# Two attentions on one core: the order table of the units is arranged anew

## The chip, the cores and the metric

The kernel runs on one core of a Trainium2 chip. The metric is device time in microseconds (us) from launch to end; less is better. Three runs of the kernel before gave 173.02, 172.65 and 172.67 us, a median of 172.67.

## The reference

Two attentions stand one behind the other. The first takes q, k, v of shape (8 batches, 8 heads, 576 rows, 64), pools k and v eightfold to 72 rows, and attends. Its output, seen as x of shape (8, 576, 512), goes into a mixture of four causal attention experts, of which each row takes the two with the largest gate logits.

```python
k_p = k.reshape(B, H, Sp, 8, D).mean(axis=3)
v_p = v.reshape(B, H, Sp, 8, D).mean(axis=3)
attn = softmax(q @ k_p.T / sqrt(D))
x = heads_side_by_side(attn @ v_p)
logits = x @ w_gate
w = softmax over the two largest logits
for e in range(4):
    a = causal_softmax((x @ wq[e]) @ (x @ wk[e]).T / sqrt(64))
    out += w[e] * (a @ (x @ wv[e]) @ wo[e])
```

## The kernel before

The 576 rows of a batch are worked as 512 main rows and 64 tail rows; the tails of two batches (b-1, b with b odd) are joined to one block of 128 rows. Matmuls are in bf16 with sums in fp32.

The work of each batch is cut into **units**, and a unit's name is `batch:unit`. The main ones:

- loads (`lk`, `lq`, `lv`, with a head group's number in batches 0 and 1; tails `lkt`, `lqt`, `lvt`; weights `W:lq`, `W:lk`, `W:lv`, `W:lo`), all issued on SyncE's queue (SP)
- `ks`, `vs`: first sums of the pooling, on GpSimd (POOL) from batch 2 on, on VectorE (DVE) and POOL before; `kt`, `vt`, `qt`, `qc`: casts to bf16 on POOL (`qc` in batches 0 and 1 on DVE and ScalarE, ACT); `W:c0` to `W:c3`, `W:cv`, `W:co`: casts of the weights on ACT
- `kp`, `vp` (line 362, 378): the pooling ends as matmuls, copied out by DVE
- `q0` to `q3` (396): four transposes, copied out by DVE; `s0` to `s3` (419): scores of the first attention, two 512-wide matmuls with 64 rows of contraction each, then one exponential on ACT (`etA`); `a0` to `a3` (432): eight matmuls, then DVE divides by the sums (`rzA`, `x_tm`)
- `x0` to `x3` (464): transposes of x, copied by DVE; in batches 6 and 7 the DMA does it (`xd`)
- `p0` to `p3` (512): projections to query and key, four 512-wide matmuls with `wqk`, copied out by ACT (`qk`); `v0`, `v2` (527): values and gate logits, eight 260-wide matmuls, copied out by DVE
- `g1` to `g6`: the gates
- `c00`, `c01`, `c10`, `c11`, `c2` (645, 656): scores of the experts, matmuls with 64 rows of contraction, an exponential on ACT and the causal mask on POOL (`etB`, `etC`); `o0`, `o1` (665): twenty matmuls, scaled by DVE; `t0`, `t1` (699, or by DMA in batches 4 to 6): transposes; `w`, `y`, `z` (719, 728): the output projection, copied out by ACT or DVE, and stored
- `qx`, `sx`, `ax`, `xx`, `pt`, `vx`, `h0`, `h1`, `hd`, `ox`, `tx`, `w4` (756 to 960): the same for the joined tails
- `W:h0` to `W:h31` (287): **empty units**, two 512-wide matmuls on a tile of zeros each, whose result is not used.

The units `s`, `c`, `sx`, `h0`, `h1`, `hd` contract over 64 rows, in pairs: one matmul in rows 0 to 63 of the array, one in rows 64 to 127. The profile shows them as `64*128` and this document calls them **row-tiled**; all other matmuls are **full**.

A unit is a Python generator with up to three stages: its matmuls, the reading of their result by ACT or DVE, and what follows (a mask, a store). The string `ORDER` (line 21) names a unit once for each stage. The last lines of the kernel (986 to 991) walk through it:

```python
parts = {}
for name in ORDER.split():
    if name not in parts:
        parts[name] = units[name]() or iter(())
    next(parts[name], None)
```

So the first mention of a unit issues its matmuls, the second the copy or the exponential, the third the mask or the store. Every instruction goes through a wrapper that keeps the program's order (126 to 141; for that reason nearly all lines of the profile are L134), and each engine works off its own in that order. `ORDER` is thus the queue of every engine at once, SP's too. Waits follow from data and from buffers: results of matmuls lie in two rings of PSUM, `ps1` with 2 buffers (`kp`, `vp`, `q`, `x`, `p`, `t`, `w`, `y`, `qx`, `xx`, `pt`, `vx`, `ox`, `tx`, the empty units) and `ps2` with 3 (`s`, `a`, `v`, `c`, `o`, `z`, `sx`, `ax`, `h0`, `h1`, `hd`), lines 145 and 146. A unit that takes a buffer waits until the unit that had it before has been read. The raw inputs have two buffers of each kind (148).

Of the kernel before, what the change touches and what calls it, by code (L numbers as in the profile page):

```python
# [43 lines left out]
3:x1 1:ox 3:x3 3:x1 4:s1 3:x3 W:lo 4:s3 4:s0 4:s3 3:x0 4:vp 3:x0 5:ks 3:pt 3:pt 4:s2 4:vp 5:kt 2:c11
4:s2 3:x2 2:c00 5:q2 2:g3 1:o0 3:x2 2:c11 1:o1 3:p3 4:a3 5:q2 5:q3 3:p3 3:hd 5:lv 5:lvt 1:o1 2:c2
5:q1 5:q3 2:g4 3:p2 4:a3 2:c2 3:hd 4:a0 5:q1 4:a0 5:qt 2:c11 3:p1 2:c2 4:a1 2:c01 3:p2 5:vs 6:lq
4:a1 3:c10 2:c10 3:p1 1:t1 3:vx W:co 3:vx 1:t1 6:lk 3:v0 3:c10 5:q0 3:p0 5:q0 0:w0 4:a2 3:hd 2:c10
3:v0 2:g5 2:c10 3:c11 0:w0 3:h0 5:kp 3:p0 4:a2 5:qx 3:c11 3:v2 5:kp 5:qx 0:w3 3:h0 2:g6 3:v2 0:w3
5:vt 6:lvt 5:s3 5:s1 4:x0 5:s3 1:t0 6:qc 7:lvt 2:o0 4:x0 4:x2 1:t0 5:s1 0:w2 4:x2 2:o0 5:sx 3:g1
0:w2 5:vp 5:vp 3:g2 4:x1 7:kt 5:s0 6:lv 0:w3 5:sx 7:vt 3:c2 2:o1 4:x1 6:q3 6:q3 4:x3 5:s0 4:x3 3:g3  # L50
2:o1 3:c2 5:ax 0:w1 4:p1 5:ax 0:w1 4:p1 2:t0 3:h1 2:t0 6:lkt 7:lk 3:c10 5:s2 6:q1 5:s2 6:q1 5:a0
6:vt 4:p0 6:q0 6:q0 6:ks 4:v2 6:vs 5:a0 3:h1 2:t1 4:p0 2:t1 4:p3 6:kt 1:w3 4:p3 5:a2 5:a1 3:g4 4:p2
7:lq 4:v2 1:w3 5:xx 5:a2 5:a1 4:p2 3:c01 5:xx 3:c00 6:kp 3:c01 3:c00 5:a3 6:kp 5:pt 0:w1 7:ks 6:q2
4:c01 5:a3 6:s3 3:c2 4:c00 6:q2 5:pt 1:tx 0:w2 1:tx 6:vp 5:x0 3:g5 4:c01 4:v0 1:w3 4:c00 5:x0 6:s3
2:w1 6:vp 6:lqt 2:w1 0:w0 5:x1 3:c11 4:v0 6:s1 6:s0 3:g6 5:x1 5:x3 4:g1 7:qc 3:c00 5:x2 5:x3 3:o1
7:lqt 6:s1 4:g2 1:w4 6:a3 6:s0 5:x2 2:w0 3:c01 7:lv 1:w4 2:w0 6:a0 3:o1 6:a3 5:p3 7:q2 4:c2 5:p3
6:a0 4:c00 7:qt 1:w4 7:q2 4:c11 6:s2 7:kp 2:w0 4:c2 6:s2 4:c01 3:ox 7:kp 7:q3 5:v0 7:q3 6:a2 3:ox
2:w2 5:p2 5:v0 4:c11 2:w2 5:vx 4:c10 6:a2 7:vs 7:s3 5:vx 4:c2 6:a1 5:p2 4:c10 1:w2 2:w3 4:g3 5:v2
1:w2 6:a1 5:v2 2:w3 1:w0 3:t1 5:h1 2:w2 7:s3 3:t1 7:s2 5:hd 6:xd0 7:q1 4:c10 7:q1 1:w0 5:h1 5:hd
6:xd3 5:p1 3:o0 1:w0 5:g1 7:vp 3:o0 7:s2 5:c10 4:g4 6:xd1 7:vp 4:g5 5:g2 5:p1 5:c10 4:g6 7:s1 7:s1  # L60
5:g3 7:q0 4:o0 6:xd2 5:p0 7:q0 7:a3 5:g4 5:hd 4:o0 1:w1 7:a1 5:p0 1:w1 7:qx 7:a3 2:w1 7:qx 5:c2 7:a1
7:s0 3:tx 7:s0 6:p3 3:tx 7:a2 2:w3 1:w2 5:c2 6:p1 7:a0 7:a2 7:a0 5:g5 4:c11 1:w1 7:sx 6:p3 5:h0 6:p0
6:v2 6:p1 3:w4 4:t0 5:h0 7:sx 3:w4 6:v2 7:ax 7:xd2 4:o1 6:p2 6:p0 7:ax 3:t0 5:c11 4:o1 6:p2 3:t0
5:c11 7:xd3 5:g6 5:c01 5:c00 7:xd0 3:w3 5:c10 3:y1 3:w3 7:xd1 5:c11 6:v0 3:y1 3:w0 5:c2 6:v0 5:c00
3:w0 5:ox 6:c00 4:t1 5:ox 6:c2 7:xx 5:c01 7:v0 6:g1 6:c2 6:g2 4:w2 3:y1 6:c00 5:o1 7:xx 3:w2 7:v2
# [956 lines left out]
```

## Time and profile before

| | |
|---|---|
| median of three runs | 172.67 us (172.65 to 173.02) |
| span of the profiled execution | 171.8 us |
| time of the runs beside that span | 0.9 us more |
| TensorE matmul (PE) busy | 160.6 us, 94% |
| ACT busy | 125.1 us, 73% |
| DVE busy | 124.3 us, 72% |
| POOL busy | 100.8 us, 59% |
| empty matmuls | 61 records, 18.2 us busy |
| DMA | 42.03 MB, mean 245 GB/s |
| granted TensorE clock | 1.00 |

The profile comes from one execution; its times count from the first instruction, and its span leaves out what lies around the program's instructions, so the runs are a little longer. PE is TensorE's matmuls, PEld its weight loads, which overlap. A row of the timeline gives the start, the length, the engine, line, operation, what is written and read by the program's names, the shape and the number of merged instructions; in brackets stands idle time ahead of it and what ended that. The chain of waits goes back from the last instruction to what released it each time. A matmul's record is longer than the distance to the next matmul's start, since they are pipelined (26 of the 2,090 matmuls have no record).

### The profile page before, as it was taken

To read this page: it belongs to the slowest core of one execution; us is meant where nothing else is said; L and a number is where in the kernel's file an instruction comes from. 1 tells how busy PE (TensorE), PEld (TensorE's weight loads), DVE (VectorE), ACT (ScalarE), POOL (GpSimd) and SP (SyncE) were. 2 spreads that over 40 slices of the span, in tenths; PEclk is the share of its full clock that TensorE was granted. 3 is DMA by queue.
4 is the path that set the end of the run, shared out by engine and by line. 5 is a ranking of instruction groups with operands and counts; after the bars stand their busy time and mean duration, and the time that the engine had idled before them with its cause. 6 is when DMAs were issued, how large, how long until landed. Compare 5 with 4: busy or idle time off the path is not lost.

```text
span 171.8 us, 5246 instructions
## 1 busy us (share of the span) xinstructions
PE 160.6 (94%) x2064; PEld 101.7 (59%) x2090; DVE 124.3 (72%) x358; ACT 125.1 (73%) x176; POOL 100.8 (59%) x222
## 2 busy tenths in 40 slices
...
GB/s 140 262 342 335 306 301 257 332 335 329 216 321 347 332 332 301 295 287 334 302 82 341 360 216 201 230 126 61 67 122 275 65 125 156 210 216 132 333 253 208
DMA packets 52712, 42.03 MB, mean 245 GB/s; under 512 B 21712, under 2 KB 47824, under 8 KB 52688
## 3 DMA queue, kind: packets, MB, share of 16 engines
...
HBM read 30.42 MB, written 9.44 MB: 232 GB/s over the span
## 4 chain that ended last, share of the span: by engine, by line
PE 75%; DVE 7%; ACT 6%; DMA 4%; SPq 3%; issue 2%; DVEq 0%; ACTq 0%
PE p_ps L134 14%; PE v_ps L134 8%; PE y_ps L134 7%; PE sB_ps L134 5%; PE oB_ps L134 5%; PE sA_ps L134 4%; PE qT_ps L134 4%; DMA qraw<-in_q_dram 4%; PE idle_ps L134 4%; PE oA_ps L134 4%; PE xT_ps L134 3%; SPq L134 3%; PE oBt_ps L134 3%; PE vp_ps L134 2%; PE pt_ps L134 2%
## 5 line engine op out<-in xcount | busy, mean ns | idle before, releaser
L134 ACT ACTIVATE etA<-sA_ps 72x1024 bf16<-72x1024 f32 x32 | 31.3, 1018 | 10.7 <-PE sA_ps L134 10.5
L134 PE MATMUL p_ps<-xT,wqk 128*128 128x512 bf16 x114 | 31.5, 379 | 1.5 <-ACT qk L134 0.6
L134 ACT ACTIVATE etB<-sB_ps 128x1024 bf16<-128x1024 f32 x32 | 32.2, 1025 | 0.2 <-PE sB_ps L134 0.2
L134 POOL TENSOR_SCALAR_AFFINE_SELECT etB<-etB 128x256 bf16<-128x256 bf16 x48 | 18.8, 410 | 12.2 <-ACT etB L134 11.8
L134 POOL TENSOR_TENSOR vsum<-vraw 128x512 bf16<-128x512 f32 (+2 forms) x18 | 18.3, 1041 | 9.9 <-DMA vraw<-in_v_dram 9.8
L134 ACT CAST qk<-p_ps 128x512 bf16<-128x512 f32 x32 | 18.5, 586 | 7.6 <-PE p_ps L134 6.8
L134 DVE TENSOR_TENSOR x_tm<-oA_ps,rzA 128x512 bf16<-128x512 f32 x32 | 22.1, 692 | 1.1
L134 PE MATMUL idle_ps<-idle 128*128 128x512 bf16 x61 | 18.2, 414 | 3.1 <-DVE kp L134 1.3
L134 PEld LDWEIGHTS <-wqk 128*128 128x128 bf16 x192 | 14.7, 98 | 10.4 <-issue 1.1
L134 DVE COPY qT<-qT_ps 128x512 bf16<-128x512 bf16 x32 | 15.4, 487 | 6.2 <-PE qT_ps L134 5.9
L134 POOL TENSOR_TENSOR ksum<-kraw 128x512 bf16<-128x512 f32 (+1 forms) x16 | 18.0, 1146 | 2.3 <-DMA kraw<-in_k_dram 2.3
L134 PE MATMUL y_ps<-wo_t,oT 128*128 128x512 bf16 x57 | 16.7, 379 | 0.2
L134 PE MATMUL v_ps<-wvg,xT 128*128 128x260 bf16 x128 | 16.8, 274 | 0.0
L134 ACT COPY ofin<-y_ps 128x512 f32<-128x512 f32 x20 | 11.6, 587 | 6.4 <-PE y_ps L134 1.7
L134 POOL CAST qbf<-qraw 128x2048 bf16<-128x2048 f32 x6 | 11.4, 1897 | 5.6 <-ACT etT L134 5.5
L134 PEld LDWEIGHTS <-xT 128*128 128x128 bf16 x128 | 11.9, 97 | 3.1 <-issue 0.4
L134 PEld LDWEIGHTS <-etA 72*128 72x128 bf16 x256 | 11.0, 97 | 4.3 <-DVE x_tm L134 0.4
L134 PE MATMUL sB_ps<-qk 64*128 64x512 bf16 (+3 forms) x128 | 13.2, 299 | 0.0
L134 PEld LDWEIGHTS <-etB 128*128 128x128 bf16 x256 | 11.3, 97 | 2.5 <-POOL etB L134 0.6
L134 DVE COPY xT<-xT_ps 128x512 bf16<-128x512 bf16 x24 | 9.7, 420 | 4.1 <-PE xT_ps L134 3.8
L134 PE MATMUL oB_ps<-vaug,etB 128*128 128x65 bf16 x256 | 12.4, 193 | 0.1
L134 PE MATMUL qT_ps<-ident,qbf 128*128 128x128 bf16 x128 | 12.2, 219 | 0.3
...
## 6 DMA issues: line engine op xcount, KB each, us to landing
...
```

Source lines behind the costliest of these rows:

```text
L134: return tc.keep_in_program_order(fn(*args, **kwargs))
```

## The change

Only the string `ORDER` changes: the same units, with the same stages, in another order. Nothing is added and nothing taken away; shapes, buffers, engines and the code of the units stay. The new order comes from a search on a model with durations taken from a trace, which charges for each change between full and row-tiled matmuls. Since the table is the order of all queues, the order of the loads changes too, and the places of the empty units. The first 20 lines and the last 6 of the old table, then the first 21 and the last 6 of the new:

```diff
@@ -19,58 +19,58 @@
 ORDER = """
-W:h21 W:h22 W:h7 0:lk3 W:h3 0:lq3 0:lkt 0:ks3 0:kt 0:qc3d 0:lk2 W:h18 0:lk0 W:h14 W:h16 0:lv1 W:h27
-0:lvt 0:qc3a W:h28 0:lq0 W:h13 0:kp3 0:lq2 0:lk1 W:h30 0:q3 0:vs1 1:lq1 0:lq1 0:kp3 0:qc0a 1:lkt
-0:ks2 W:h12 W:h25 0:vt 1:qc1a 0:qc0d 0:lv2 0:q3 0:s3 0:qc2a W:h4 0:s3 0:qc1a 0:vs2 0:ks0 0:kp2 W:h9
-W:h1 0:kp2 0:ks1 1:qc1d 0:qc2d 0:kp0 0:lv3 W:h26 0:kp1 0:kp0 W:h19 0:lv0 W:h15 0:kp1 0:q0 0:vs0 W:h5
-0:qc1d 0:q2 0:q0 1:lq0 W:h8 0:q2 1:kt 0:vs3 0:q1 1:q2 0:q1 0:s0 0:s1 0:s0 0:s2 1:lk1 0:vp 1:q2 0:s2
-1:lk0 1:lvt 0:vp 1:ks1 0:lqt W:h23 1:lv1 1:q3 0:a0 1:lv0 0:a2 1:q3 W:lk 1:qc0d 1:ks0 1:lqt W:h6 0:s1
-0:a1 1:vt W:lq 0:a2 0:a0 1:qc0a 0:a1 W:h29 1:q1 W:h11 W:h17 W:h2 1:q1 1:kp1 1:kp0 1:kp1 1:vs0 1:kp0
-0:a3 1:q0 0:a3 1:s2 1:qt 1:s1 1:q0 W:lv 0:x0 1:s0 1:s2 0:x2 2:lq 1:s1 1:s3 2:qc 1:s0 0:x0 W:c1 0:x2
-0:x1 W:h10 W:h0 1:vs1 W:h20 W:h24 1:s3 0:x3 0:x1 1:vp 0:x3 W:c3 0:p1 2:lkt 1:vp W:c2 0:p1 1:qx 1:qx
-1:a1 1:a3 1:a0 W:c0 0:p3 1:a1 1:sx 1:a3 0:p3 W:cv 2:kt 0:p0 1:a0 2:lk 1:a2 0:p2 0:v2 1:a2 1:sx 0:v0
-0:p0 1:x3 0:p2 0:c2 1:x1 0:v2 0:c2 0:c11 0:v0 1:x3 1:x2 0:c11 0:c2 0:c10 1:x1 2:lv 2:lvt 1:x2 0:g1
-0:c00 0:g2 0:c11 2:q0 2:q0 1:x0 1:x0 1:ax 2:q1 2:q1 1:ax 1:p1 1:p2 0:c00 0:c01 2:ks 3:lk 0:g3 0:g4
-1:v2 3:lkt 1:p1 2:q3 1:v2 2:vs 2:q3 1:p2 2:lqt 2:kp 0:c01 1:v0 3:lqt 1:xx 2:kp 0:g5 3:lq 2:vt 3:lvt
-2:s1 0:c10 0:c10 1:xx 2:s1 1:v0 2:s0 2:q2 1:vx 2:q2 2:s0 2:s3 2:s3 0:g6 2:s2 2:s2 3:lv 2:vp 4:lq
-0:c00 1:vx 1:g1 0:o1 1:g2 2:vp 1:p3 2:a1 1:g3 2:a2 0:o1 3:ks 3:qt 0:c01 2:a1 1:p3 1:pt 2:a2 4:lkt
-2:a0 1:p0 3:kt 1:pt 2:a3 2:a0 2:a3 4:lk 4:lvt 3:qx 1:g4 1:hd 1:h0 3:qx 3:qc 1:p0 1:hd 3:kp 1:h0
-1:c11 3:kp 1:c2 2:x2 2:x1 3:vs 2:x2 3:vt 4:lv 1:c11 2:x1 0:o0 1:c2 2:x0 0:o0 2:x3 1:c00 2:x0 3:sx
-2:x3 1:c00 1:c10 3:q2 3:q3 3:sx 2:v2 4:qc 3:q2 3:q3 0:t1 5:lq 1:c10 1:g5 3:q1 0:t1 4:kt 3:q1 3:s3
-2:v2 2:v0 0:t0 2:v0 3:s3 3:s1 3:s2 0:t0 3:q0 3:s1 1:h1 3:vp 3:q0 2:p1 3:s2 1:hd 4:lqt 3:vp 3:s0
-7:lkt 1:c01 4:q2 2:g1 1:h1 2:g2 1:c00 2:p1 4:q2 3:s0 3:a1 5:lkt 2:p0 4:q1 1:c2 3:a1 4:ks 4:q1 3:a3
...
-7:p0 3:w3 4:y0 5:t1 6:c11 6:g6 7:c11 7:c10 5:t0 6:c00 6:o1 4:y0 5:tx 7:p0 7:c10 7:c11 6:c01 7:p1
-6:o1 4:y1 5:tx 6:o0 5:w4 7:p1 5:y1 7:c11 7:c2 7:g4 4:y0 5:w4 6:t1 7:c00 6:o0 7:c01 5:y1 6:t0 7:c2
-5:y2 7:c10 5:y2 7:pt 5:y1 5:y2 7:c2 7:c01 7:pt 5:y0 7:o1 7:g5 5:w4 7:c01 5:y0 7:g6 7:h1 5:w3 7:o1
-7:c00 6:y1 5:w3 6:y1 7:c00 7:o0 6:w0 7:h1 7:t1 7:h0 5:y0 7:o0 5:w3 7:t1 7:hd 6:w0 7:t0 6:y1 7:hd
-6:w0 6:y3 7:h0 7:hd 7:t0 6:y3 7:z2 6:y3 7:z2 7:ox 7:ox 6:w2 6:w2 7:z0 7:tx 6:w2 7:tx W:h31 7:w4 7:z0
-7:w4 7:w4
+W:h16 W:h27 0:lk3 W:h29 W:h21 W:h24 W:h5 W:h20 W:h22 0:lkt W:h23 0:lk0 W:h18 W:h15 W:h11 0:lq3 0:lq1
+0:ks0 0:lq2 W:h0 W:h6 0:lq0 0:ks3 0:qc3a W:h9 W:h10 0:lk2 0:kt 0:qc3d 0:lv0 W:h3 W:h12 W:h19 0:vs0
+0:q3 0:lv3 0:q3 W:h2 0:lk1 0:kp0 0:ks2 1:lq1 W:h26 0:kp0 0:kp3 W:h4 0:qc0a 0:qc2a 0:qc0d 0:kp3
+0:qc2d 0:lv1 0:lvt 0:qc1a 0:q0 1:qc1a 1:lkt W:h13 0:q0 W:h7 0:vt 0:lv2 0:kp2 1:lk1 1:lk0 0:kp2 1:lv0
+0:qc1d W:h25 W:h1 1:lq0 0:ks1 0:lqt 0:q1 0:q2 0:s3 0:s0 0:q1 1:lv1 0:s3 0:q2 1:qc1d W:h8 0:s2 0:kp1
+0:s2 1:kt 0:kp1 0:vs1 W:h14 0:s0 1:lvt W:h30 0:vs3 0:vs2 1:q3 0:s1 1:q3 0:vp W:h28 0:s1 0:vp 1:q2
+1:ks1 0:a2 0:a0 1:kp1 1:lqt W:lq 0:a2 0:a3 0:a0 1:ks0 0:a1 1:q2 W:lk 1:kp1 W:lv 1:s2 0:a1 1:vs0
+1:kp0 0:a3 1:qc0a 1:kp0 1:s3 1:qc0d 0:x2 1:q1 1:s2 0:x2 1:q0 1:q1 1:s3 1:vt 1:s1 1:q0 0:x1 2:lq 1:s0
+1:qt 1:vs1 2:lk 1:s1 0:x1 2:qc 1:s0 1:vp 0:x0 W:c0 W:c2 1:vp 1:a1 0:x0 1:qx 1:a1 1:a0 2:lkt 1:qx
+1:a3 0:x3 W:c1 0:x3 1:a2 2:lv 1:a3 W:c3 0:p2 2:lvt 4:lvt 1:a0 1:a2 0:p2 1:sx W:cv 0:p0 2:ks 0:p1
+0:v0 2:kt 3:lqt 3:lkt 0:p0 1:x0 0:p1 1:x0 2:lqt 0:v0 0:p3 0:c00 1:sx 0:p3 1:x1 0:c01 0:c11 1:x3
+0:c00 1:x1 1:x2 0:c01 3:lk 0:v2 3:lq 1:x3 2:q1 1:x2 2:q1 2:q0 0:c11 1:v0 2:q0 2:q3 1:p1 1:p1 2:q3
+0:v2 1:ax 0:g1 0:c11 1:v0 1:p2 2:kp 0:g2 0:c2 1:p2 2:vs 1:v2 0:g3 1:ax 2:kp 0:c2 2:s1 1:xx 2:q2 2:vt
+1:v2 0:g4 3:lv 0:c00 1:xx 2:s0 0:c10 3:lvt 2:s1 2:s0 2:q2 1:vx 1:vx 0:c10 4:lq 0:c2 2:vp 0:c10 3:qt
+2:s2 0:g5 2:s2 2:s3 2:vp 1:p3 1:p3 5:lqt 0:g6 2:a1 2:a2 3:kt 1:g1 2:a1 1:pt 2:a2 2:s3 1:c11 2:a0
+1:c11 1:p0 3:ks 2:a0 2:a3 2:a3 4:lkt 0:c01 0:o1 1:pt 3:qx 1:g2 4:lk 0:o1 3:qc 1:p0 1:h0 3:vs 3:kp
+5:lq 3:qx 0:o0 1:h0 1:c10 1:c00 3:kp 1:c10 W:h17 2:x0 1:c00 2:x3 1:hd 0:o0 1:h1 7:lqt 2:x0 5:lkt
+3:q1 4:lv 2:x3 3:vt 1:hd 2:x1 1:h1 1:c2 3:q1 2:x1 1:g3 1:g4 2:x2 3:s1 1:c11 0:t0 2:x2 3:q3 2:v2 4:qc
+0:t0 4:lqt W:lo 3:q0 3:s1 3:q3 4:vt 2:v2 3:q2 3:q2 2:v0 3:s3 2:v0 3:vp 1:c00 7:lvt 1:c2 3:sx 3:q0
+3:s3 1:c01 3:s0 0:t1 3:vp 2:p0 3:sx 3:s0 1:hd 0:t1 5:lvt 3:a1 2:g1 2:p1 2:p0 3:a1 1:g5 4:q2 5:lk
+3:s2 3:ax 4:q2 5:lv 4:q0 4:q0 2:p1 1:c01 4:ks 2:p3 4:q3 3:s2 1:c01 4:kt 3:a3 3:ax 2:p3 2:c01 3:a0
...
+4:y1 7:g1 3:w2 4:w3 7:p0 6:o1 7:p3 6:g6 5:o0 7:g2 7:p1 6:c00 7:p3 7:c10 5:tx 6:o1 5:t0 7:g3 5:tx
+6:c01 7:p1 6:o0 5:t1 5:w4 4:w3 7:c10 6:t1 7:c01 7:c11 6:o0 5:y1 7:g4 5:w4 4:y0 7:c00 7:pt 5:y1 7:g5
+7:g6 7:c11 7:c01 7:c11 7:c2 6:t0 5:y1 5:y0 5:y0 7:pt 7:c2 7:c01 7:hd 7:c10 5:y2 5:w4 5:y2 5:y0 7:c2
+7:c00 6:y1 7:o1 6:y1 6:w0 7:hd 6:y1 7:o1 7:c00 7:o0 6:w0 7:o0 5:w3 7:t1 7:hd 7:h1 7:h0 5:w3 7:t1
+6:w0 5:w3 7:t0 7:h1 7:t0 5:y2 6:y3 7:z2 6:w2 7:h0 6:y3 6:y3 7:z2 6:w2 7:ox 7:z0 7:ox 7:tx 7:tx W:h31
+6:w2 7:z0 7:w4 7:w4
 """
```

More of the change, by code (lines that the diff above doesn't have):

```diff
@@ L38 @@
-1:c11 3:kp 1:c2 2:x2 2:x1 3:vs 2:x2 3:vt 4:lv 1:c11 2:x1 0:o0 1:c2 2:x0 0:o0 2:x3 1:c00 2:x0 3:sx
-2:x3 1:c00 1:c10 3:q2 3:q3 3:sx 2:v2 4:qc 3:q2 3:q3 0:t1 5:lq 1:c10 1:g5 3:q1 0:t1 4:kt 3:q1 3:s3
-2:v2 2:v0 0:t0 2:v0 3:s3 3:s1 3:s2 0:t0 3:q0 3:s1 1:h1 3:vp 3:q0 2:p1 3:s2 1:hd 4:lqt 3:vp 3:s0
-7:lkt 1:c01 4:q2 2:g1 1:h1 2:g2 1:c00 2:p1 4:q2 3:s0 3:a1 5:lkt 2:p0 4:q1 1:c2 3:a1 4:ks 4:q1 3:a3
-2:p0 3:ax 2:p3 1:c11 1:c01 2:p3 3:a3 4:q3 2:c01 4:vt 2:c00 5:lk 1:c01 2:c01 4:q3 4:q0 3:ax 2:p2 1:g6
-3:a0 4:q0 3:a0 5:lqt 4:kp 2:p2 4:kp 3:a2 4:vs 2:c00 1:ox 5:qc 3:xx 1:c10 3:a2 3:xx 4:s1 4:s0 1:o0
@@ L44 @@
[L44 to L65, printed above, removed]
@@ new lines @@
+5:lq 3:qx 0:o0 1:h0 1:c10 1:c00 3:kp 1:c10 W:h17 2:x0 1:c00 2:x3 1:hd 0:o0 1:h1 7:lqt 2:x0 5:lkt
[3 more added lines that the diff above has]
+3:s2 3:ax 4:q2 5:lv 4:q0 4:q0 2:p1 1:c01 4:ks 2:p3 4:q3 3:s2 1:c01 4:kt 3:a3 3:ax 2:p3 2:c01 3:a0
+4:q1 4:q3 7:lkt 3:a3 4:q1 2:c01 1:ox 2:p2 3:a0 3:a2 1:c2 1:g6 2:p2 2:c00 1:ox 4:kp 3:a2 5:qc 3:xx
@@ new lines @@
+4:kp 1:o0 3:xx 2:c00 2:g2 7:lq 2:g3 6:lq 3:x3 1:c10 2:c11 3:x3 3:x1 3:x1 3:pt 2:c00 2:c11 5:q3 4:s0
+4:vs 4:s3 1:o0 3:pt 4:s3 5:q3 4:s2 3:x2 5:qt 4:vp 2:c11 4:s2 3:x2 5:q2 1:o1 4:vp 3:x0 5:q2 4:s0 3:x0
+2:g4 4:a3 3:vx 3:p3 5:kt 1:o1 2:c2 6:lqt 3:hd 3:vx 4:a3 3:p2 5:ks W:co 3:p3 4:a0 2:c2 5:q1 3:p2 4:a0
+3:hd 3:v0 5:q1 4:s1 2:c10 5:vs 1:t1 4:s1 1:t1 2:c10 3:p1 5:vt 5:q0 3:v0 3:p1 3:c11 5:q0 3:c10 4:a1
+3:c10 2:c2 4:a1 0:w0 0:w0 6:lkt 2:g5 2:c01 3:p0 4:a2 3:v2 3:p0 0:w3 4:a2 5:kp 3:h0 3:c11 0:w3 7:qt
```

21 lines of the change are left out of this document (19 added, 2 removed).

## The prediction, before the result was known

> **What bounds the kernel now.** I read the page first (busy shares, chain), then TensorE's busy time by stretch, then its timeline at 10 ns.
>
> ```profile
> span 171.8 us, 5246 instructions
> ...
> PE 160.6 (94%) x2064; PEld 101.7 (59%) x2090; DVE 124.3 (72%) x358; ACT 125.1 (73%) x176; POOL 100.8 (59%) x222
> ...
> PE 75%; DVE 7%; ACT 6%; DMA 4%; SPq 3%; issue 2%; DVEq 0%; ACTq 0%
> ```
> ```profile
> 38.80:167.60 128.80, 126.62 (x1783) 1.00 0.79 232
> ```
>
> TensorE (PE) is the bound: it holds 75% of the chain, and from 38.8 us to its last matmul it is idle for only 128.80 - 126.62 = 2.2 us. So after the start the time is a sum of what PE issues. An order cannot change which matmuls run; it can change the changes of shape between them, where the empty matmuls (the `W:h` units) stand, and the waits.
>
> A busy row hides short waits, because a matmul's record lasts longer than the distance to the next one. So I go by distances between starts:
>
> ```profile
> 96.58 0.39 PE L134 MATMUL oT_ps<-ident,o_sc 128*128 128x128 bf16 x4
> 96.90 0.41 PE L134 MATMUL sBx_ps<-qkt,qk 64*128 64x64 bf16 x16
> 97.15 0.38 PE L134 MATMUL sA_ps<-qT,kp 64*128 64x512 bf16 x2
> 97.46 0.40 PE L134 MATMUL qT_ps<-ident,qbf 128*128 128x128 bf16 x4
> 97.69 0.41 PE L134 MATMUL oA_ps<-vp,etA 72*128 72x65 bf16 x8
> 97.94 1.03 PE L134 MATMUL p_ps<-xT,wqk 128*128 128x512 bf16 x4
> 98.80 0.39 PE L134 MATMUL qT_ps<-ident,qbf 128*128 128x128 bf16 x4
> 99.03 0.50 PE L134 MATMUL v_ps<-wvg,xT 128*128 128x260 bf16 x3
> ```
>
> Four full transposes followed by a full matmul take 99.03 - 98.80 = 0.23 (0.22 in most such rows, the price used); four followed by a row-tiled one (`64*128`) take 96.90 - 96.58 = 0.32. A full 512-wide matmul takes (98.80 - 97.94)/4 = 0.215; a row-tiled pair runs as one, and followed by a full one it takes 97.46 - 97.15 = 0.31. So **one change of shape, in either direction, costs 0.095 us** of PE, and tiled after tiled (96.90 to 97.15, sixteen small matmuls) pays nothing. Nothing else waits in these rows.
>
> The Trainium skill, page "TensorEngine Tiling (Array Packing)", section Key Properties, says the same in kind: "Mode switching requires drain". It gives no figure there; "TensorE: Matmul & The Clock Gate" puts the drain at about 128 cycles of 2.4 GHz, an estimate of 0.053 us a change, by which the term of changes below would be 0.85 instead of 1.52 and the forecast 173.4. The rows have the duration, so they decide.
>
> **The change, part by part.** Only the table moves; every instruction, load and tile stays. A unit's matmuls are issued at its first mention, so PE's order can be read off: of 364 units with matmuls, 88 are row-tiled (`s`, `c`, `sx`, `h`). The old table has them in 46 runs (12 single, 26 pairs, 8 threes): 92 changes. The new one has 56 runs (29 single, 22 pairs, 5 threes): **112 changes**. That a search charged for them does not alter the count: 20 more, 20 x 0.095 = 1.9 us.
>
> *The start.* I compare the moment when `0:c11` begins, the first stretch in which PE runs dense. Before:
>
> ```profile
> 29.39 0.62 ACT L134 CAST wqk<-vraw 128x512 bf16<-128x512 f32 x1 [1.25 <-DMA vraw<-in_moe_wk_dram]
> ...
> 31.59 0.62 ACT L134 CAST wqk<-vraw 128x512 bf16<-128x512 f32 x1 [0.15 <-DMA vraw<-in_moe_wq_dram]
> ```
> ```profile
> 27.78 1.46 PE idle_ps L134 x6
> 29.24 0.22 PE xT_ps L134 x4
> 29.46 0.66 PE vp_ps L134 x4
> 30.12 0.98 PE p_ps L134 x4
> ...
> 36.19 1.79 PE v_ps L134 x16
> ```
> ```profile
> 38.79 0.39 PE L134 MATMUL sB_ps<-qk 64*128 64x384 bf16 x4
> ```
> ```profile
> 30.16 0.69 DVE L134 CAST vp<-vp_ps 72x512 bf16<-72x512 f32 x1 [0.24 <-PE vp_ps L134]
> 31.43 0.42 DVE L134 COPY qTt<-qTt_ps 128x512 bf16<-128x512 bf16 x1 [0.58 <-PE qTt_ps L134]
> 31.77 0.20 DVE L134 RECIPROCAL rzA<-oA_ps 128x8 f32<-128x8 f32 x1
> 32.00 0.69 DVE L134 TENSOR_TENSOR x_tm<-oA_ps,rzA 128x512 bf16<-128x512 f32 x1
> 32.61 0.20 DVE L134 RECIPROCAL rzA<-oA_ps 128x8 f32<-128x8 f32 x1
> ```
>
> Until 29.4 PE waits for the weights and fills time with empty matmuls: that work is free only there. (The first fence is ACT's timeline, the second the chain, the third PE's timeline at `0:c11`.) The loads ahead of the weights are the same in both tables but for one more 128 KB tail ahead of the first weight. The old order has that tail between the two weights, 640 KB that take the 2.2 us from 29.39 to 31.59, so the tail is worth 0.44 by bytes; its rows are short, so I allow twice that: the first weight lands at about 30.3, the second at 31.5 as before. Casts `c0`, `c2` are done at 31.4. Nineteen instead of eleven empty units now stand ahead of the first transposes; they delay PE at the very start, but the batch-1 work behind them still waits for its loads.
>
> On VectorE (DVE) the new table has, in a row, `1:vp` (0.69), `0:x0`, `1:a1`, `1:qx`, `0:x3`, `1:a3`, `1:a0`, with 0.84 for each `a` (31.77 to 32.61) and 0.42 for each copy. `1:vp` needs the last v loads of batch 1, which land ahead of the weights, so some 2 us before 29.4 or a little later: on PE at about 27.6 (0.66, chain above), copied at 29.0; `a1`'s first pass follows at about 29.7, and so x3 is copied at 31.4 and a0's buffer free at 33.0. With 0.86 for a projection, 0.90 for half of the values (half of 1.79), 0.22 for transposes and for a tiled pair of this width, 0.24 for `oA` or 16 small tiled ones and 0.095 a change, PE runs: `0:p2` 31.5, `1:sx` 33.1 (it waits for a0's buffer, 0.6), `0:p0` 33.4, `0:p1` 34.3, `0:v0` 35.1, `1:x0` 36.0, `0:p3` 36.2, `0:c00` 37.2, `1:x1` 37.5, `0:c01` 37.8, `0:c11` 38.0. Against 38.79: **-0.8**. Bounds: 37.4 if a0's buffer is free in time (-1.4), 39.0 if DVE runs one us later (+0.2).
>
> *What PE still owes from there*, new less old:
> - useful work: old has done `0:v2`, `1:x3`, `0:c2` (0.90 + 0.22 + 0.22), new instead `0:c00`, `0:c01`, `1:x0` (0.66): **+0.68**.
> - changes of shape: 19 of 112 done, 93 left, against 92 - 15 = 77 left: 16 x 0.095 = **+1.52**.
> - an empty unit: `W:h17` moved from the start to just ahead of `2:x0`, some 17 us into the dense stretch: 2 x 0.215 = **+0.43**. Its old cover was the wait for weights; there is none here unless `2:x0` would wait (then 0).
>
> Sum without waits: -0.8 + 0.68 + 1.52 + 0.43 = **+1.8**.
>
> *Waits.* Of the 128.8 us, distances between starts less the prices above leave 4.8 us of waits in the old order, 2.2 of it visible as idle; 22 places over 0.06 make 3.6 of it, the rest is rounding of the rows. They sit where ScalarE (ACT) gets several exponentials at once:
>
> ```profile
> 54.51 1.02 ACT L134 ACTIVATE etX<-sBx_ps 128x1024 bf16<-128x1024 f32 x1
> 55.44 1.02 ACT L134 ACTIVATE etB<-sB_ps 128x1024 bf16<-128x1024 f32 x1
> 56.34 1.03 ACT L134 ACTIVATE etC<-sB_ps 128x1024 bf16<-128x1024 f32 x1
> 57.24 1.04 ACT L134 ACTIVATE etB<-sB_ps 128x1024 bf16<-128x1024 f32 x1
> ```
>
> Four of them, without idle between, keep ACT for 3.8 us. With such durations laid along each table (ACT's and DVE's work that PE's units release, less the time that PE takes over them), ACT's largest surplus over PE's time in one stretch after the start is 4.2 us in the old table and 3.7 in the new; DVE's are 2.8 and 2.7. So the new one is a little more even. Against that stands the tail:
>
> ```profile
> 164.94 1.46 PE L134 MATMUL y_ps<-wo_t,oT 128*128 128x512 bf16 x5
> ...
> 166.24 0.28 PE L134 MATMUL oTt_ps<-ident,o_st 128*128 128x128 bf16 x2
> ...
> 166.89 0.70 PE L134 MATMUL yt_ps<-wo_t,oTt 128*64 128x512 bf16 x4
> ```
>
> Between the end of `7:ox` (164.94, where `y_ps` follows) and `7:tx` (166.24) DVE scales `7:ox`'s result. The old order fills these 1.3 us with `6:w2` and `7:z0` (six matmuls, 6 x 0.215 = 1.29) and hardly waits, so DVE needs about that long; the new one issues `6:w2` ahead of `7:ox` and has only `7:z0`: 0.4 of wait, and behind it stand `W:h31` and the last matmuls. The rest of the end (167.6 to 171.8, copies and stores) is alike. I take -0.8 for evener ACT and +0.4 for the tail: **-0.4**. Bounds: all waits over 0.06 gone, -3.6; waits two thirds more, +3.2.
>
> Sum: **+1.4 us** (1.8 - 0.4) on the profiled span, 171.8 to 173.2. The median shown, 172.67, lies 0.9 over that span; the same 0.9 is added, so 172.67 + 1.4 = **174.1**.
>
> **Rivals.**
> *B, evener load wins (faster).* The waits of ACT go almost wholly. For it: the ACT rows above, and the smaller surplus. Against it: the distances from a unit to the next use of its buffer are as short in the new table as in the old (a full transpose unit reused after 0.63 in both). Time: 1.8 - 3.3 = -1.5, 171.2. It decides once more than 2.1 us of waits vanish.
> *C, GpSimd (POOL) feeds PE late (slower still).*
>
> ```profile
> 49.96 2.49 POOL L134 TENSOR_TENSOR ksum<-kraw 128x512 bf16<-128x512 f32 x2
> ```
>
> The old POOL begins batch 3's k sums at 49.96 without idle before them. The new table puts four 128 KB tails (`4:lvt`, `3:lqt`, `3:lkt`, `2:lqt`) ahead of batch 3's k load on SP's queue and `3:qt`, `3:kt` and two more masks ahead of the sums on POOL; `3:ks` then runs about 50.3 to 52.8, and `3:kp` is due at 53.5. Cover: 0.7. If POOL is 3 us later, PE loses 2.3: 172.67 + 1.4 + 2.3 = 176.4.
> *D, the drains fall into waits.* The 16 extra changes cost nothing where PE would wait anyway. For it: some follow transposes whose consumer is late. Against it: PE waits 2% of the stretch. Time: 174.1 - 1.5 = 172.6, no change.
> *E, the change does as it says:* fewer drains, so faster by their price. The count excludes it; no chance.
>
> **How the numbers follow.** Forecast 174.1: 0.52, its own range 172.9 to 176.0. B 0.22, C 0.14, D 0.12. The range takes in B's middle and C's: 171.2 to 176.9 leaves out the outer half of B and the far part of C, under 0.2. The three runs shown span 0.2%, so 0.2% (0.35 us) is what can be told from no change. Faster: B and 0.03 of the forecast's lower end, 0.25. Same: most of D, 0.10. Slower: the rest, 0.65.
>
> **What would show it.** Each change at 0.09 to 0.10 in the new starts, and 112 of them; `0:c11` near 38.0 and `1:sx` waiting for a DVE copy; two idle matmuls near 55 us with no wait beside them; a gap of about 0.4 ahead of `oTt_ps`; PE's idle share after 39 us near 2%. Wrong: `0:c11` beyond 39, more than 3 us of visible idle after it, or waits under 2 us by starts (B).

## The result, and the profile after

The new order takes **180.33 us** (median of five runs, 179.72 to 181.61) against 173.02 for the old one on the same chip (172.65 to 173.26): a ratio of **1.0419**, 95% interval 1.0386 to 1.0452. It is slower, as forecast, and beyond the range: 174.1 was forecast, 176.9 the upper end. The profiled execution of it is the longest of the five, 181.61 us (span 179.9); the spans of the other four are 178.0 to 178.7. So the medians lie 7.3 us apart and the profiled spans 8.1. In every run that lists both, the time is 1.7 to 2.0 us more than the span; the 0.9 us of the table before is therefore not a constant of the program, and by these 1.7 us the old order's profiled execution, 171.8, was about 0.8 us slower than the median (an estimate).

The page of the new order: span, busy times, the slices of TensorE (PE) and of its granted clock, and the chain.

```profile
span 179.9 us, 5278 instructions
...
PE 168.1 (93%) x2090; PEld 103.4 (57%) x2090; DVE 126.4 (70%) x358; ACT 126.2 (70%) x176; POOL 100.3 (56%) x222
...
PE   7999769999999999999999999999999989988990
...
PEclk9999995599999999999999999999999999999999
...
PE 79%; DVE 10%; DMA 4%; ACT 3%; issue 1%; DVEq 0%; SPq 0%; ACTq 0%
```

The matmuls are the same, and yet PE is busy for 168.1 us instead of 160.6. The clock's row shows about half of the reason: two of the forty slices stand at 5, half speed, where the old order had full speed from 4.9 us on. (At full clock, with a record for each of the 2,090 matmuls, the same table with three empty units moved is busy for 164.2: e7 below.) DMA holds 4% of the chain as before; then it was the load of q, now 3% of it are transposes, `oT<-o_sc`.

The stretch from `0:c11` to the last matmul, PE alone (length, busy, records, clock, DMA share, GB/s), and the timeline at `0:c11`:

```profile
42.00:175.70 133.70, 130.67 (x1816) 1.00 0.76 216
```
```profile
41.79 0.61 PE L134 MATMUL sB_ps<-qk 64*128 64x384 bf16 x8
```

The second row holds `0:c01` and, 0.22 later, `0:c11`: it begins at 42.0 and not at 38.0. From there on the clock is full, and visible idle is 3.0 us instead of 2.2. By distances between starts, with the prediction's prices, waits after 40 us are 7.0 us in the new order and 4.8 in the old. So the terms are:

| term, us of span | predicted | measured |
|---|---|---|
| `0:c11`, against 38.79 | -0.8 | +3.2 |
| owed from there: changes 1.52, useful work 0.68, `W:h17` 0.43 | +2.63 | +2.63 by count |
| waits from there (2.2 by starts; the rest behind the last matmul) | -0.4 | +2.3 |
| sum | +1.4 | +8.1 (179.9 - 171.8) |

**Where the clock fell.** PE in five windows of 3.4 us of the new order, and then the old order at the same stage:

```profile
19.60:23.00 3.40, 2.24 (x20) 1.00 1.15 281
23.00:26.40 3.40, 1.97 (x44) 1.00 1.19 258
26.40:29.90 3.50, 3.25 (x20) 0.51 1.10 339
29.90:33.30 3.40, 3.04 (x22) 0.50 1.11 337
33.30:36.70 3.40, 3.40 (x38) 0.50 1.13 341
```
```profile
18.50:22.00 3.50, 3.39 (x42) 1.00 1.21 272
22.00:25.40 3.40, 3.23 (x34) 1.00 1.08 313
25.40:28.80 3.40, 2.97 (x24) 1.00 1.17 245
```

The clock is granted in full from 5.97 to 26.45 us, then halved for 10.24 us, then full again. Ahead of the fall PE is busy 2.24 and 1.97 of 3.4 us; the old order has 2.97 or more there. The timeline says what made the gap (PE's waits, a projection mostly at half clock, and one row of VectorE, DVE):

```profile
20.73 0.38 PE L134 MATMUL vp_ps<-vsum,pm 128*128 128x512 bf16 x1 [0.84 <-DVE vsum L134]
...
24.20 0.42 PE L134 MATMUL oA_ps<-vp,etA 72*128 72x65 bf16 x8 [0.34 <-DVE x_tm L134]
25.58 0.39 PE L134 MATMUL sA_ps<-qT,kp 64*128 64x512 bf16 x2 [0.96 <-DVE kp L134]
...
35.38 1.67 PE L134 MATMUL p_ps<-xT,wqk 128*128 128x512 bf16 x4
```
```profile
18.62 2.70 DVE L134 TENSOR_TENSOR vsum<-vraw 128x128 bf16<-128x128 f32 x4
```

Nineteen empty units ahead of `0:q3` put the first transposes at 11.8 us (8.2 in the old order), DVE's sums of v follow late, and PE waits for DVE again and again with few empty units left to fill it. The four matmuls of a projection then take 1.67 us instead of 1.03.

**The late waits.** Rows of the new order's PE timeline, and one of its chain:

```profile
145.62 0.59 PE L134 MATMUL y_ps<-wo_t,oT 128*128 128x512 bf16 x2 [0.73 <-ACT ofin L134]
...
162.57 0.39 PE L134 MATMUL y_ps<-wo_t,oT 128*128 128x512 bf16 x1 [1.13 <-DMA oT<-o_sc]
...
173.11 1.03 PE L134 MATMUL y_ps<-wo_t,oT 128*128 128x512 bf16 x4
174.27 0.29 PE L134 MATMUL oTt_ps<-ident,o_st 128*128 128x128 bf16 x2
```
```profile
157.99 4.53 DMA oT<-o_sc
```

By starts, `3:w0` to `3:w3` loses 0.89 (ACT copies `3:w0` late, and its PSUM buffer is the one `3:w3` needs), `5:y1` loses 1.31 (a transposing DMA lands 4.5 us after its issue, where four of the other five of its kind take 2.4), `5:y2` and `5:w3` 0.26 and 0.37, and the tail 0.30 (`7:z0` at 173.11, `oTt_ps` at 174.27: 1.16 for four matmuls of 0.215).

### The profile page after: what moved, and what is told of

It is laid out like the page before. It is cut to its first block, busy times and chain, and to the rows that moved or that the text cites. A ratio compares the mean times of both kernels' runs of the same rounds, so it can differ in the third digit from the quotient of the medians.

```text
span 179.9 us, 5278 instructions
## 1 busy us (share of the span) xinstructions
PE 168.1 (93%) x2090; PEld 103.4 (57%) x2090; DVE 126.4 (70%) x358; ACT 126.2 (70%) x176; POOL 100.3 (56%) x222
## 4 chain that ended last, share of the span: by engine, by line
PE 79%; DVE 10%; DMA 4%; ACT 3%; issue 1%; DVEq 0%; SPq 0%; ACTq 0%
PE p_ps L134 14%; PE idle_ps L134 9%; PE v_ps L134 8%; PE y_ps L134 6%; PE sB_ps L134 5%; PE sA_ps L134 5%; PE oA_ps L134 4%; PE qT_ps L134 4%; PE oB_ps L134 4%; PE xT_ps L134 4%; DMA oT<-o_sc 3%; PE oBt_ps L134 2%; PE vp_ps L134 2%; PE pt_ps L134 2%; DVE x_tm L134 2%; DVE o_sc L134 2%
## 5 line engine op out<-in xcount | busy, mean ns | idle before, releaser
L134 ACT ACTIVATE etA<-sA_ps 72x1024 bf16<-72x1024 f32 x32 | 31.6, 1017 | 8.1 <-PE sA_ps L134 7.7
L134 PE MATMUL p_ps<-xT,wqk 128*128 128x512 bf16 x128 | 33.2, 385 | 0.0
L134 PE MATMUL y_ps<-wo_t,oT 128*128 128x512 bf16 x64 | 18.4, 379 | 1.9 <-DMA oT<-o_sc 1.1
L134 PEld LDWEIGHTS <-etA 72*128 72x128 bf16 x256 | 11.7, 102 | 4.3 <-issue 1.2
L134 PE MATMUL oA_ps<-vp,etA 72*128 72x65 bf16 x256 | 13.5, 200 | 0.7 <-ACT wqk L134 0.4
L134 PE MATMUL sA_ps<-qT,kp 64*128 64x512 bf16 x64 | 11.7, 404 | 1.1 <-DVE kp L134 1.0
```

The lines of the kernel that those rows point to most:

```text
L134: return tc.keep_in_program_order(fn(*args, **kwargs))
```

## The experiments

Times are medians with the ratio to the kernel before on the same chip. "Waits" are those after 40 us, by starts, of the profiled execution, of which each kernel has one. With the same table up to `0:c11`, that moment lies at 38.12 to 38.83 us in three executions (the old order, e3, e4) and at 36.98 to 37.91 in five (e1, e5, e9, e10, e12), so a difference under a us there says nothing by itself.

### Is it the clock? (e1, e7, e11, e2)

e1 moves six empty units from the front into the gap:

```diff
-0:ks0 0:lq2 W:h0 W:h6 0:lq0 0:ks3 0:qc3a W:h9 W:h10 0:lk2 0:kt 0:qc3d 0:lv0 W:h3 W:h12 W:h19 0:vs0
+0:ks0 0:lq2 0:lq0 0:ks3 0:qc3a 0:lk2 0:kt 0:qc3d 0:lv0 W:h19 0:vs0
...
-0:vp 1:q2 1:ks1 0:a2 0:a0 1:kp1
+0:vp 1:ks1 0:a2 0:a0 W:h0 W:h6 W:h9 1:q2 1:kp1
...
-1:qc0d 0:x2
+1:qc0d W:h10 0:x2
-1:s0 1:vp 0:x0
+1:s0 W:h3 W:h12 1:vp 0:x0
```

> The new order with six of its empty units moved from the front into the stretch from 22 to 31 us (three behind 0:a0, one ahead of 0:x2, two ahead of 1:vp, and 1:q2 behind the first three). Theory clock (PE had too little to do from 19.6 to 26.4 us, so the granted clock fell to 0.5 for 10.24 us): clock 1.00 throughout, 0:c11 at about 38.5 instead of 42.0, time about 177 (180.33 less 3.5). Rival queue (the start is late because DVE's queue is, and the clock only slows what would wait anyway): full clock or not, 0:c11 stays at 41 or later and the time above 179.3.

Measured: 177.12, ratio 1.0246 (1.0191 to 1.0302). The clock is full throughout, `0:c11` begins at 37.4, waits are 7.0. The same work, empty units included, is some 3 us faster because it is spread. Two things changed at once: PE begins the transposes earlier (`0:q3` at 8.3 instead of 11.8), and the gap is filled.

e7 moves only `W:h0`, `W:h6`, `W:h9` to behind `0:a0`, with `1:q2` behind them.

> The new order with only three empty units moved, from the front to behind 0:a0 (and 1:q2 behind them), 1.3 us of matmuls in the stretch from 23.0 to 26.4 us in which the clock was lost. Theory clock: the stretch's share of streaming matmuls rises from 0.36 to about 0.7, and the clock does not fall at 26.4; if later stretches hold by themselves (0.64 of a halved clock there), it stays at 1.00 and the time is 177 as in e1. If the waits from 26 to 31 us are as bare, it falls one or two stretches later and the time is 179 or more.

Measured: 177.86, ratio 1.0293 (1.0242 to 1.0344); clock full, `0:c11` at 37.8. PE in the two emptiest of its windows, laid on its own grant (6.38 us):

```profile
23.50:26.90 3.40, 2.39 (x28) 1.00 1.17 247
26.90:30.30 3.40, 2.64 (x28) 1.00 1.11 341
```

The emptiest has 2.39 instead of 1.97: with three empty units, 1.3 us of work, in the gap the clock holds. `1:s2`, which begins at 25.58 in the new order (the row above with 0.96 of wait), shows how the loss divides; in e7:

```profile
23.72 0.39 PE L133 MATMUL sA_ps<-qT,kp 64*128 64x512 bf16 x2
```

The new order is 1.9 us behind e7 there, ahead of the clock's fall, and 4.2 behind at `0:c11` (42.0 against 37.8). So less than half of the delay was there before the clock fell, and 2.3 us came in the halved stretch.

e11 leaves those six units out altogether, twelve empty matmuls fewer, and puts nothing in the gap.

> The new order without the six empty units W:h0, W:h6, W:h9, W:h10, W:h3, W:h12 of the start: twelve empty matmuls are left out, and nothing stands in the gap. It tells apart the two things that e1 and e7 did at once (empties out of the front, empties into the gap). Theory (the clock falls where TensorE streams too little for a whole window): batch 1's loads still set the pace, the gap of 19 to 27 us stays unfilled, the granted clock falls for 6.8 to 10.2 us, 0:c11 at 40 to 42, time 178.5 to 180.5. Rival (the empties' delay of the first transposes makes the gap): the clock holds, 0:c11 near 37.5, time 177 to 177.5.

Measured: 178.37 (176.90 to 178.88), ratio 1.0270 (1.0215 to 1.0325). The clock falls in every run (mean 0.965 to 0.981), in the profiled one from 21.65 for 6.83 us:

```profile
18.20:21.60 3.40, 2.33 (x45) 1.00 1.15 338
21.60:25.10 3.50, 2.96 (x22) 0.51 1.18 248
```

So taking the empties out of the front doesn't hold the clock; that takes filling in the gap. But by the medians it saves about as much: by ratio (1.0270) e11 can't be told from e7 (1.0293) or e1 (1.0246), whose intervals overlap with its own. The profiled execution, 176.90 us and the shortest of its four, has `0:c11` at 37.4 with the clock halved for 6.83 us, since PE begins early (`0:q3` at 8.5) and much of the halved stretch lies over waits. The rival was right on that place, the theory on the clock, and the median lies between the two (177.7 if the ratio is taken to 173.02). The fallen clock is costly where PE is late already; the late start and the fall cost what they do together.

e2 takes the **old** order and moves ten empty units (`W:h23`, `h6`, `h29`, `h11`, `h17`, `h2`, `h10`, `h0`, `h20`, `h24`) from its gaps to the front.

> The old order with ten empty units that stood between 19 and 29 us moved to the front, so that the waits there are bare. Theory clock: the granted clock falls to 0.5 in the start of this order too, and the time is 2 to 4 us over 173.0. Rival queue: empty units stand only where PE would wait, so the clock stays at 1.00 and the time within 0.5 us of 173.0.

Measured: 176.15, ratio 1.0176 (1.0119 to 1.0232). Waits stay at 4.7, `0:c11` slips to 42.4 (and `0:q3` from 8.2 to 13.3), and the clock falls for 6.83 us:

```profile
23.90:27.30 3.40, 1.47 (x34) 1.00 1.14 302
27.30:30.70 3.40, 2.89 (x28) 0.50 1.11 312
```

The places of the empty units alone, with every other unit where it was, cost the old order 3.3 us; here too the late first transposes and the bare gap come together.

### What does a change of shape cost? (e3)

The old order with ten full units moved one place forward, each between two row-tiled ones, so that 92 changes become 112 and hardly anything else moves. Three of the ten, in the order of PE's units:

```diff
-3:c10 2:c10 1:t1
+3:c10 1:t1 2:c10
-5:s3 5:s1 4:x0
+5:s3 4:x0 5:s1
-2:s1 2:s0 2:q2
+2:s1 2:q2 2:s0
```

> The old order with ten full units moved one place forward, each between two row-tiled ones, so that it has 112 changes of shape as the new order has, and all else as before. Theory price (0.095 us for each change, nothing hides it): 173.0 + 20 x 0.095 = 174.9, clock 1.00. Rival hidden (the drains fall into waits): below 173.5.

Measured: 174.87 against 172.80, ratio 1.0104 (1.0066 to 1.0142). In the profiled pair `0:c11` is 0.67 earlier (38.12, within the scatter named above) and the last matmul ends 1.23 later (168.82 against 167.59): -0.67 + 20 x 0.095 = 1.23, so the waits are the same in both. The price holds, and rival D, that the changes fall into waits, does not.

### Are the waits the new order's own? (e4, e6, e8)

e4 has the old table as far as `2:q0`, and the rest in the new order.

> The old order up to the first stage of 2:q0 (40 us), and from there all that is left in the new order: 110 changes, no empty unit after the start but W:h31. Theory own waits (the 7.0 us of waits that the new order has after 40 us, against 4.8, belong to it): 173.0 + 18 x 0.095 + 2.2 = 176.9. Rival aftermath (they follow from the clock's fall at the start, by which loads, stores and engines were out of step): 173.0 + 1.7 = 174.7.

Measured: 178.69, ratio 1.0331 (1.0290 to 1.0372), clock full, `0:c11` at 38.8 as in the old order, waits 7.9. It is slower than expected: with the old start and a full clock the new rest still loses 3 us of waits against the old one. The waits belong to the new order from there on.

e6 is the reverse: e1's start as far as `2:q1`, `W:h17` at the front, then the old order.

> The start of e1_new_empties_in_gap up to 2:q1, W:h17 put to the front too, and from there the old order: 94 changes. If the new start is good once its clock holds and the loss lies in the rest: 0:c11 at 37.4, waits after 40 us near 4.8, time 172.8 - 1.4 + 0.7 - 0.2 = 171.9, under the old order. Rival (the new start leaves loads and casts behind, which the old rest pays for): 173.5 or more.

Measured: 173.18, ratio 1.0002 (0.9976 to 1.0028), waits 4.7. `0:c11` is at 38.1, and the last matmul ends only 0.3 earlier than before (167.29). Of the new start no gain can be seen.

e8 is e1 with `W:h17` back at the front instead of ahead of `2:x0`.

> e1_new_empties_in_gap with W:h17 taken from ahead of 2:x0 to the front. Theory term (an empty unit in the dense stretch costs its 0.43 us): 177.1 - 0.4 = 176.7, PE's end 0.4 earlier. Rival cover (2:x0 would wait anyway): 177.1.

Measured: 177.10, ratio 1.0244 (1.0208 to 1.0280), as e1. PE with and without the unit (e1 first, then e8):

```profile
54.79 0.39 PE L134 MATMUL idle_ps<-idle 128*128 128x512 bf16 x1
55.23 0.61 PE L134 MATMUL xT_ps<-perm,x_tm 128*128 128x128 bf16 x8
55.92 0.29 PE L134 MATMUL sBd_ps<-qkt 64*128 64x128 bf16 x4
```
```profile
55.60 0.62 PE L133 MATMUL xT_ps<-perm,x_tm 128*128 128x128 bf16 x8
56.74 0.29 PE L133 MATMUL sBd_ps<-qkt 64*128 64x128 bf16 x4 [0.52 <-DVE o_sc L133]
```

Without it `1:hd` waits 0.52 for DVE, and it begins as far behind `0:c11` as in e1 (18.57 us in both). The unit filled a wait and cost nothing there; the +0.43 of the prediction was covered.

### Where do the late waits come from? (e5, e9, e10, e12, e13, e14)

e5 is e1 with the copy of `3:y1` ahead of that of `3:w0`, `5:y1` behind `7:pt`, and `6:w2` behind `7:ox`.

> e1_new_empties_in_gap with three places mended: 3:y1's copy ahead of 3:w0's (so that 3:w3 gets the buffer of 3:y1 and not that of 3:w0), the matmuls of 5:y1 behind 7:pt (its transposes by DMA land late), 6:w2 behind 7:ox as in the old order. Theory buffers and queue (a unit gets the ps1 buffer that comes free first in the program's order, and 5:y1 waits for SP's queue): the 0.89, 1.3 and 0.30 us of waits there go, PE's waits after 40 us fall from 7.0 to about 4.6, time 177.1 - 2.4 = 174.7. Rival bunching (the waits come from ACT's and DVE's backlog): they appear at the next units, time above 176.3.

Measured: 177.19, ratio 1.0261 (1.0185 to 1.0337), waits 6.8. (It has 110 changes of shape, two fewer than e1.) The waits mended are gone and others stand in their place, `5:y2` with 0.82 the largest. DVE shows a new releaser:

```profile
162.46 0.69 DVE L134 COPY ofin<-y_ps 128x512 f32<-128x512 f32 x1 [1.12 <-DMA out_dram<-ofin]
```

A copy waits for one of the four output buffers, whose stores stand on SP behind the transposing DMAs.

e9 takes e1 and asks whether the store issued right behind `5:t1` delays its landing:

```diff
-5:t1 5:w4 4:w3 7:c10 6:t1 7:c01
+5:t1 5:w4 7:c10 6:t1 4:w3 7:c01
```

> The new order with its start filled (as e1, 177.1), and one store moved: that of 4:w3 stands behind 6:t1 on SP's queue instead of between 5:t1 and 6:t1. Theory (a store issued right behind a DMA transpose delays its landing): oT of 5:t1 lands in 2.5 to 3 us instead of 3.7 to 4.5, the wait of 5:y1 falls from 1.3 to below 0.5, and the time falls by 0.5 to 1.0, to about 176.3. Rival (the landing time of a transpose does not depend on what is queued behind it, 5:y1 simply stands too early): the wait of 5:y1 stays near 1.3, time 177.1. Second rival (backlog): the wait of 5:y1 falls and reappears at 5:y2 or 5:w3, which wait for output buffers, time 177.0.

Measured: 177.33, ratio 1.0229 (1.0184 to 1.0275). `5:y1` still waits 1.33 and its DMA takes 4.55: the theory fell.

e10 adds to e9 the copy of `3:y1` ahead of that of `3:w0`, and other output buffers for batch 5:

```diff
-            t = ofp.tile([128, DM], FP32, name="ofin", tag="ofin")
-            copy(out=t[:], in_=ps[:])
+            if b == 5:
+                if "vo" not in st:
+                    st["vo"] = rawp.tile([128, H, NR * D], FP32, name="vraw", tag="vraw")
+                t = st["vo"][:, 2 * c : 2 * c + 2, :].rearrange("p h n -> p (h n)")
+            else:
+                t = ofp.tile([128, DM], FP32, name="ofin", tag="ofin")[:]
+            copy(out=t, in_=ps[:])
```

> As e9, and besides the copy of 3:y1 ahead of that of 3:w0, and batch 5's outputs (y0, y1, y2, w3) are copied to a free buffer of the raw inputs instead of the ring of four output buffers. Theory (the late waits come from two buffers given back late and from a ring of four output buffers whose stores stand behind transposes): 3:w0's 0.89 and 5:y2's 0.26 and 5:w3's 0.35 vanish, waits after 40 us fall from 7.0 to about 4.5 to 5, the time is about 175.0 to 175.5, which leaves the 20 changes and the start. Rival (backlog: a wait that is taken away comes back at the next unit, as in e5): waits after 40 us stay at 6.5 or more, time 176.5 to 177.

Measured: 176.14, ratio 1.0175 (1.0116 to 1.0233), waits 5.75. `3:w0` and `5:w3` no longer wait, `5:y2` by 0.20, so 1.1 us (6.9 to 5.75) came from buffers given back late; `5:y1` still waits 1.17. The intervals of the ratios of e9, e10, e12 and e13 overlap, so from here on gains of about 1 us are read from the profiled executions.

e12 is e10 with the third transpose, `6:t1`, behind the store of `4:y0`.

> As e10, and the issue of 6:t1, the third DMA transpose of oT within four us, stands behind the store of 4:y0 (some 3 us later) instead of right behind 5:t1. Theory (5:t1's oT lands late, 4.4 us after its issue, because a third transpose is queued while it is under way): 5:t1's oT lands within 2.4 to 2.7 us, the issue of each transpose on SP takes 1.2 us instead of 2.4 for the third, the wait of 5:y1 (1.2 in e10) vanishes, time 175.0. Rival (the landing of 5:t1 does not depend on it, or the wait reappears because oT of batch 6 is late now): 5:y1 still waits 1.2, or 6:y1 and 6:w0 wait instead; time 176.1 or more.

Measured: 176.74, ratio 1.0224 (1.0168 to 1.0280). The third one's issue now takes 1.2 us, but `5:t1` still lands after 4.40 and `5:y1` still waits 1.18. This theory fell too.

The cause stands in the trace's semaphore records. The sixteen completions of `5:t1`'s DMA, one for each DMA engine, in e12 (us):

```
154.35 154.36 154.37 154.39 154.40 154.41 154.43 154.44
154.45 154.47 154.48 154.49 154.51 154.52 154.53 156.47
```

One of the sixteen is 1.94 us late. At that time a transfer of another kind is under way, 16 KB of **instructions** from 153.98 to 155.39, and the last two packets of the transpose start as it ends, at 155.38 and 155.39. (The records don't name the engine of a packet; that both lie on one engine is read from these times.) In the new order itself such a transfer runs from 159.95 to 161.44, and the sixteenth completion comes at 162.53, the others by 160.46. The old order has one too, at 154.02, but it falls on a store, for which nobody waits. The page's part on DMA, for e10 from 154 to 157 us:

```profile
q8 instruction: 1, 0.02, 2.9%
...
oT<-o_sc SPq DMA_TRANSPOSE x2, 4.0
```

2.9% of sixteen engines over 3 us is 1.4 us of one engine. e13 and e14 move that transfer and leave the order alone: as e10, with 51 and 12 small empty matmuls more in the gap of the start, so that PE's instructions come that much later in the program.

```diff
-    def busy():
+    def busy(small=0):
...
+        for _ in range(small):
+            pe.matmul(
+                out=ps[:, 0:64], lhsT=idle[:, 0:128], rhs=idle[:, 0:64], start=True, stop=True
+            )
...
-        units[f"W:h{n}"] = busy
+        units[f"W:h{n}"] = lambda n=n: busy(17 if n in (0, 6, 9) else 0)
```

> As e10, and the three empty units in the gap of the start issue 51 more small empty matmuls (64 columns each), so that 102 more instructions of PE stand ahead of all that follows. Theory (5:t1's oT is late because a transfer of 16 KB of instructions, one for each 256 instructions of PE or about 9.9 us, holds one of the 16 DMA engines for 1.4 us just then, and its last completion comes 1.1 us after that transfer's end): that transfer now starts 102/256 of 9.9, or 3.9 us earlier against the units, before oT's packets; all 16 completions of 5:t1's oT come together, the wait of 5:y1 falls from 1.17 to below 0.2, waits after 40 us from 5.75 to about 4.6, and the time is 175.0 if the 1.4 us of small matmuls lie in the waits of the gap, 176.0 if they cost half. Rival (the landing has another cause): 5:y1 still waits 1.2 and one completion of oT still comes 1.9 us after the others.

> As e13 with 12 small empty matmuls, 24 more instructions of PE: the transfer of instructions starts 24/256 of 9.9, or 0.9 us earlier. Theory: it still overlaps the packets of 5:t1's oT, but ends 0.9 us earlier, so the last completion comes 1.0 instead of 1.9 us after the others and 5:y1 waits about 0.25 instead of 1.17; time about 175.2. Rival: the wait stays at 1.2, time 176.1.

Measured: e13 175.86, ratio 1.0149 (1.0082 to 1.0215), waits 4.9; e14 (4 in place of 17) 175.21, ratio 1.0102 (1.0038 to 1.0165), waits 5.3. The same part of the page and PE's row of `5:y1` in e13 (one fence each):

```profile
q1 hardware_dynamic: 1225, 0.29, 48.3%
...
oT<-o_sc SPq DMA_TRANSPOSE x2, 2.5
```
```profile
156.63 0.60 PE L134 MATMUL y_ps<-wo_t,oT 128*128 128x512 bf16 x2
```

No transfer of instructions in that stretch, 2.5 us to landing, all sixteen completions of `5:t1` within 0.2 us, and `5:y1` does not wait. e14 has them within 0.2 us too, and waits 0.26 for a landing of normal length (2.47 us): its transfer falls on the issue of `5:t0`, which takes 2.23 us instead of 1.22, and `5:t1` stands behind it. The transfer starts at 154.74 in e10, at 151.06 in e13 and at 151.43 in e14; with `0:c11` at 37.67, 38.11 and 37.04 that is 4.1 us earlier against the units in e13, as expected, and 2.7 in e14, not 0.9. What sets the moment of the transfer stays open.

Two runs above show the same with no edit at all behind the start. In e7 and e11 the transfer begins 0.3 us later against `0:c11` than in e1, just behind the last packets of `5:t1`. That lands after 2.47 us in both, and `5:y1` doesn't wait. But the issue of `6:t1`, under way by then, takes 2.4 us instead of 1.2, `6:t0` stands behind it on SP, and PE waits at `6:y1` instead (by starts 1.1 in e7 and 1.2 in e11, against 0.26 in e1). Two rows of e7:

```profile
156.86 0.60 PE L133 MATMUL y_ps<-wo_t,oT 128*128 128x512 bf16 x2
...
161.32 0.61 PE L133 MATMUL y_ps<-wo_t,oT 128*128 128x512 bf16 x2 [0.92 <-DMA oT<-o_sc]
```

From `0:c11` to the last matmul e7 and e11 take 133.4 and 133.5 us, e1 133.6: a few tenths decide which DMA the transfer meets, and PE pays about as much for either.

## Why the prediction was wrong, and where it was right

- **The empty units of the start** are the step that failed: "they delay PE at the very start, but the batch-1 work behind them still waits for its loads", and that the old order's empty matmuls are work that "is free only there". They were priced as time, and as time that a wait would cover. Neither held. Ahead of the clock's fall PE waits for DVE (0.84, 0.34 and 0.96 us in the rows above) and not for loads, and at `1:s2` it is 1.9 us behind e7. And the empty matmuls also hold the clock: with those at the front spent early, the gap of 20 to 26 us halved it, and in the halved stretch PE fell 2.3 us further behind. These 4.2 us make +3.2 at `0:c11` out of e7's -1.0; -0.8 was forecast, with a bound of +0.2. That the places of the empty units do it is shown by e1, e7 and e2; e11 shows that the fall alone, without the late start, does not move `0:c11`. What a full clock would have left of the 1.9 us is not shown, nor how much of the medians' loss belongs to each of the two: one of the new order's five executions has a mean clock of 0.990, which is 1.8 us lost to the clock in all, and yet a span of 178.1.
- **With the clock held the working gives the right place:** 38.0 predicted, 37.8 in e7, 37.0 to 37.9 in the executions with e1's start; `0:p2` at 31.5, 31.6 in e7. Its weights come too late, though (the casts `c0` and `c2` end at 30.0 in e1, not at 31.4); that this does not show is luck, since DVE's copy of `0:x3`, for which `0:p2` waits too, ends at 31.4 there.
- **Waits, -0.4,** failed in sign: +2.3. The comparison of ACT's and DVE's surplus counted the work that PE releases, but not who holds a buffer, nor what else a DMA engine carries. The new order issues `5:y1` and `5:y2` close behind what they need; 1.1 us came from buffers (e10), and the collision of one DMA with a transfer of instructions cost 1.2 at its place; when the transfer was moved away, 0.8 (5.75 to 4.9, e13) and 0.45 (e14, where it meets another issue) was left as a gain. The tail's +0.4 came out as 0.30. By itself +2.3 lies inside the bound of +3.2 that the prediction gave for waits; it was the start that took the time out of the range.
- **Changes of shape** were right in count and price: 20 for 1.9 us (e3). That the table was made by a search that charges for them did not show in their number.
- **`W:h17`**, +0.43, was mis-sized: it was covered (0), as the prediction's own exception allowed (e8).
- **The rivals.** B, evener load, is refuted by the waits. C, POOL feeding late, did not occur: no wait of 0.15 us or more stands at `3:kp` in the new order. D fell with e3. The upper end of the range was made from C, a late engine, and held no case in which the clock falls.

With the clock held and the late waits mended, e14's span is 173.2, which is the span that was forecast; but that is luck. It is made of -1.75 at `0:c11` (37.04, at the low end of the scatter; -0.8 was forecast), +2.63 owed and +0.5 of waits (-0.4 was forecast): two errors that cancel. e14 differs from the new order in its empty matmuls, in batch 5's output buffers and in the places of three stages. None of the versions tried is faster than the kernel before; e6 equals it.
